# One listed order for a sorted-block attention and its two-layer network: chunk 0's queries on both row halves, keys copied whole, the second sort matrix computed later

## The chip, the core and the metric

The kernel runs on one core of a Trainium2 chip. A core has a matrix engine (TensorE, in the profile PE; its weight loads are shown apart as PEld), a vector engine (VectorE, DVE), an engine for activation functions (ScalarE, ACT), a general engine (GpSimd, POOL) and one that mostly issues transfers (SyncE, SP). Each engine takes its own instructions strictly in the order of the program, and waits on semaphores for what others have to finish first. TensorE reads SBUF and writes PSUM; VectorE and ScalarE move results from PSUM back to SBUF. Transfers are issued from the queues of POOL, SP and ACT; here POOL issues those that also convert float32 to bfloat16.

The metric is device time in microseconds (us) of one execution. The times are those of whole executions; the profile is of one execution and shows its span, from the first instruction to the last.

## The reference: what is computed

There are 4 batches of 8 heads with 768 positions of 64 features. The positions of a head are cut into 8 blocks of 96. A small 8 x 8 matrix per head is normalised five times (softmax along the rows, then division by the column sums), and mixes the blocks of keys and values. Each block of queries then attends to the one mixed block in its place. The result, 3072 tokens of 512 features, goes through a two-layer network with the activation h cos h.

```python
for _ in range(5):
    P = P - max(P, -1); P = exp(P)
    P = P / (sum(P, -1) + 1e-9); P = P / (sum(P, -2) + 1e-9)
k_sorted = einsum('bhij,bhjcd->bhicd', P, k_b); v_sorted = einsum('bhij,bhjcd->bhicd', P, v_b)
attn = softmax(scale * q_b @ k_sorted^T); x = attn @ v_sorted      # per block of 96
h = x @ w_in; out = (h * cos(h)) @ w_out                            # 512 -> 2048 -> 512
```

## The kernel before, in words

**Tiles.** The 3072 tokens are done in 8 chunks of 384: chunk n is batch n // 2, and its half n % 2 of four blocks u = 0 to 3. Per chunk and block the steps are `qk` (scores of 8 heads, maximum and subtraction on DVE), `expo` (the exponential on ACT), the transposition of the probabilities (on PE with a copy, `p_transpose`, for chunks 0 and 1; by a transposing transfer from SP after that), `av` (times the values, and the division on DVE), and the transposition of the result into `xT`. Then come the layers: `moe_up` (16 blocks f of 128 hidden features; PE products `h`, cosine on ACT as a sine with a shift, product `gg` on DVE) and `moe_down` (three tiles of 128 tokens, 16 products of 512 columns each into `o`, a copy and a store).

**Sorting.** `k_sort_0` (batch 0), `k_sort_1` (batch 1) and `k_sort_g` (batches 2 and 3 together) mix the keys by PE products with a block-diagonal matrix `bds`, 16, 8 or 4 positions of a block at a time, and copy the results into `kTs`, from which scores take their moving operand. `v_sort_b` and `v_sort_g` do the same to the values, reading for most of them `vperm`, a copy of the values with features outermost that POOL makes (`v_permute`, about 2.8 us per instruction). The two sort matrices, group 0 (batches 0 and 1) and group 1 (batches 2 and 3), are computed side by side at the start, four rounds each of exponential (ACT), column sums (a float32 product `sk` on PE) and normalisation (four small DVE instructions).

**Zeros.** A score product takes 128 rows: two heads of 64 features. To get one head alone, from chunk 1 on, the queries lie in `q_turned` with zeros in the other head's rows, one copy for each head of a pair (so 8 products of 96 columns per block); POOL writes those zeros (L658 to L661), and the transposing transfer of the queries moves them too. For chunk 0 the products use 64 rows, and `k_sort_0` writes its copies in four parts by row halves.

**What sets the order.** It is written out by hand. The scheduler is off: each engine executes in the order in which the program's calls emit instructions. `moe_up` and `moe_down` take lists of slots; after each step of the layer the calls of one slot are emitted. So a layer's slots decide where the next chunk's attention stands in each engine's queue. PSUM has three buffers of two banks (`big`, called B) and two of one bank (`acc`, C), taken in turn; an instruction that takes a buffer waits until its previous content has been read.

**Start.** POOL issues the loads of chunk 0's queries, batch 0's keys and values, three quarters of `w_in`, then (behind `v_permute`) the last quarter, chunk 1's queries, the four quarters of `w_out`, and batch 1's keys and values. PE begins with 16 products of zeros (`keep_warm`, 25 in all). Chunk 0's first layer begins when two of its four blocks are attended; it is done in two halves of 192 tokens, and the other two blocks, chunk 1's keys and chunk 1's queries stand in its slots. Chunk 1's probabilities, its values and batch 1's keys stand in chunk 0's second layer.

```python
    moe_up(0, [[(p_transpose, 0, 2, V, *C)], [(p_transpose, 0, 3, V, *C)],
               [(av, 0, 2, True), (k_sort_0, 1, 0, 16, A, *C)], [(av, 0, 3, True)],
               [(x_transpose, 0, 2, A, *C)],
               [(x_transpose, 0, 3, A, *C), (k_sort_0, 1, 16, 16, V, *C)],
               [(q_transpose, 1, 0, (V, V), *C)], [(k_sort_0, 1, 32, 16, A, *C)]],
           0, 2 * blk)
```

## Time and profile before

| what | value |
|---|---|
| time, three executions | 246.4, 247.95, 249.35 us (median 247.95) |
| the profiled execution | span 246.5 us; the page gives no other time for it |
| PE busy | 232.0 us, 94% of the span |
| DVE, ACT, POOL busy | 175.5, 158.2, 88.2 us |
| start of chunk 0's first layer | 28.91 us |
| start of chunk 0's second layer | 51.65 us |
| start of chunk 1's first layer | 70.41 us |
| start of chunk 1's second layer | 83.48 us |

The starts are those of the first `h` (L556) or `o` (L580) product in the timeline. The profile is read in this order: the share of each engine over 40 slices, with the TensorE clock that was granted; then the same by the stages of the table; then the groups of instructions with their mean durations; then the chain of work that ended last, which gives the pitch of products that follow each other. A matmul's duration in a group (379 ns for 512 columns) is longer than its pitch (1.73 us for eight), because matmuls overlap.

### The profile page before, as it was taken

The numbers are of one execution on the slowest core, as the hardware profiler recorded it, in microseconds if no ns is written. First come the engines' busy times: TensorE is split into PE (matmuls) and PEld (weight loads), VectorE is DVE, ScalarE is ACT, GpSimd is POOL, SyncE is SP. The second block draws the span as 40 slices with busy tenths as digits, with TensorE's granted clock in tenths as the row PEclk, the third lists the DMA queues.
The fourth block names the chain that finished last, engine by engine and source line by source line (L and its number), as shares of the span: only waits on it lengthen the run. The fifth ranks groups of instructions, "written<-read, shape, count | busy, mean of one in ns | idle before, by whom it ended". The sixth has DMA issues, their size and how long they took to land.

```text
span 246.5 us, 5361 instructions
## 1 busy us (share of the span) xinstructions
PE 232.0 (94%) x2159; PEld 149.5 (61%) x2159; DVE 175.5 (71%) x321; ACT 158.2 (64%) x228; POOL 88.2 (36%) x105
## 2 busy tenths in 40 slices
PE   7987898878999999999999999998999999999994
...
PEclk9555569999999999999999999999999999999999
DMA  4999999994998457946697957986490580133012
GB/s 51 232 192 169 184 205 227 165 210 95 179 214 144 34 138 107 137 103 159 170 106 137 57 128 89 245 53 114 96 245 13 112 169 26 32 83 129 0 45 85
DMA packets 68313, 31.30 MB, mean 127 GB/s; under 512 B 57024, under 2 KB 63808, under 8 KB 68032
## 3 DMA queue, kind: packets, MB, share of 16 engines
...
q10 hardware_dynamic: 512, 0.20, 0.3%
...
## 4 chain that ended last, share of the span: by engine, by line
PE 77%; DVE 8%; ACT 7%; DMA 4%; issue 2%; DVEq 0%; ACTq 0%
PE h L556 33%; PE o L580 26%; PE sc L399 3%; PE av L519 3%; DMA vperm<-p_buf 3%; PE pps L506 2%; ACT p_buf L483 2%; PE ks L346 2%; DVE kTs L286 2%; ACT L483 2%; PE vs L432 1%; DVE gg L563 1%; PE xps L544 1%; PE vs L422 1%; PE sk L258 1%
## 5 line engine op out<-in xcount | busy, mean ns | idle before, releaser
L556 PE MATMUL h<-xT,w_in_t 128*128 128x384 bf16 (+1 forms) x576 | 93.4, 313 | 1.5 <-DVE gg L563 0.8
L580 PE MATMUL o<-w_out_t,gg 128*128 128x512 bf16 x368 | 87.5, 379 | 0.5 <-DVE s L455 0.5
L560 ACT ACTIVATE c<-h,half_pi 128x768 f32<-128x768 f32 (+1 forms) x72 | 59.7, 829 | 30.7 <-PE h L556 28.3
L563 DVE TENSOR_TENSOR gg<-c,h 128x768 bf16<-128x768 f32 (+1 forms) x72 | 61.3, 860 | 24.5 <-ACT c L560 24.5
L556 PEld LDWEIGHTS <-w_in_t 128*128 128x128 bf16 x576 | 53.8, 100 | 28.8 <-issue 2.5
L580 PEld LDWEIGHTS <-gg 128*128 128x128 bf16 x368 | 33.4, 98 | 33.1 <-DVE s L455 0.7
L455 DVE TENSOR_TENSOR s<-sc,mx 96x384 f32<-96x384 f32 (+1 forms) x43 | 32.2, 749 | 2.7 <-DVE mx L454 0.5
L454 DVE TENSOR_REDUCE mx<-sc 96x4 f32<-96x384 f32 (+1 forms) x43 | 31.9, 741 | 2.8 <-PE sc L399 1.9
L177 POOL COPY vperm<-kv 64x1536 bf16<-64x1536 bf16 (+1 forms) x10 | 28.0, 2840 | 1.6 <-DMA kv<-in_v_dram 1.6
L483 ACT ACTIVATE p_buf<-s 96x768 bf16<-96x768 f32 x32 | 27.6, 895 | 0.6 <-DVE s L455 0.2
L528 DVE TENSOR_TENSOR xn<-av,r 96x512 bf16<-96x512 f32 x32 | 22.0, 686 | 1.1
L284 ACT CAST kTs<-ks 128x512 bf16<-128x512 f32 (+2 forms) x31 | 14.1, 456 | 6.1 <-PE ks L346 6.0
L134 POOL DMA_DIRECT2D kv<-in_q_dram x24 | 16.0, 676 | 3.9 <-DMA kv<-in_v_dram 3.2
L399 PE MATMUL sc<-kTs,q_turned 128*128 128x96 bf16 x224 | 16.1, 206 | 0.8 <-DVE s L455 0.7
L526 DVE RECIPROCAL r<-av 96x8 f32<-96x8 f32 x32 | 6.4, 198 | 13.8 <-PE av L519 13.7
L399 PEld LDWEIGHTS <-q_turned 128*128 128x128 bf16 x224 | 12.8, 98 | 4.8 <-DVE s L455 1.3
L284 ACT COPY o_s<-o 128x512 f32<-128x512 f32 (+2 forms) x11 | 5.9, 537 | 14.8 <-PE o L580 11.8
L284 ACT COPY kv<-o 128x512 f32<-128x512 f32 x8 | 4.7, 582 | 14.0 <-PE o L580 14.0
L134 POOL DMA_DIRECT2D q_mem<-in_q_dram x16 | 10.6, 670 | 0.3 <-issue 0.3
L560 ACT ACT_TABLE_LOAD x8 | 10.3, 1283 | 0.1
L284 ACT CAST pair<-vs 96x512 bf16<-96x512 f32 (+1 forms) x12 | 8.7, 727 | 2.0 <-PE vs L432 2.0
L519 PEld LDWEIGHTS <-pT 96*128 96x128 bf16 (+1 forms) x160 | 7.9, 106 | 3.1 <-issue 0.7
...
## 6 DMA issues: line engine op xcount, KB each, us to landing
...
kv<-in_k_dram POOLq DMA_DIRECT2D x2, 768.0 KB, 13.4
kv<-in_v_dram POOLq DMA_DIRECT2D x2, 768.0 KB, 16.6
pair<-in_k_dram POOLq DMA_DIRECT2D x2, 768.0 KB, 12.2
...
```

What stands on the lines that cost most here:

```text
L134: nc.gpsimd.dma_start(out=q_heads[:, i, :, e], in_=src[:, ih * IC + i, :, e])
L177: nc.gpsimd.tensor_copy(dst, src)
L284: eng.copy(dst, src)
L399: nc.tensor.matmul(out, q_of(n, hp)[:, x:x + 128], keys_of(n, u, h2, hp), start=True, stop=True)
L454: nc.vector.reduce_max(mx[:], scv, axis=AX.X)
L455: nc.vector.tensor_tensor(s_t[n, u][:, part[0]:part[0] + w], scv, mx.to_broadcast([blk, w, H2, blk]), op=ALU.subtract)
L483: nc.scalar.activation(dst, src, AF.Exp, scale=scale)
L528: nc.vector.tensor_tensor(xn.rearrange("p h e d -> p e h d"), avv[:, :, :, :D], r.to_broadcast([blk, 2, H2, D]), op=ALU.mult)
L556: nc.tensor.matmul(h[:, f2, :w], w_in_t[:, kk, f * 128:(f + 1) * 128], xT[n][:, kk, lo:hi], start=(kk == 0), stop=(kk == KC - 1))
L560: nc.scalar.activation(c[:, :, :w], h[:, :, :w], AF.Sin, bias=half_pi[:, 0:1])
L563: nc.vector.tensor_tensor(gt[n, fp][:, :, lo:hi], c[:, :, :w], h[:, :, :w], op=ALU.mult)
L580: nc.tensor.matmul(o[:], gt[n, f // 2][:, f % 2, ts * 128:(ts + 1) * 128], w_out_t[:, f, :], start=(f == 0), stop=(f == FC - 1))
```

## The change

The hand-written calls and slots are replaced by one list, `PLAN`, of 657 small steps, each a short text with its arguments: the letter V or A is the engine of a copy, B or C the PSUM pool. The program goes through it and calls the step's function, so an engine's order is the order of the list. `ld_` steps are loads on POOL, `z_` steps fill zeros and constants, `w N` is N products of zeros of 256 columns, `b_` steps are the sort matrix of one group, `up n f0 nf lo hi` is nf hidden blocks of the first layer for tokens lo to hi of chunk n, `dn n ts part` a quarter (four products) of the second layer's tile ts. Beside the order, these things change:

- The first loads are batch 0's values, then chunk 0's queries, then the keys; the quarters of the weights are in the order w_out 3, w_out 1, w_in 0, chunk 1's queries, w_out 2, w_in 2, w_in 1, w_in 3, w_out 0. Chunk 1's queries have a buffer of their own.
- Chunk 0: queries (`q0`) and sorted keys (`k0`) lie on both row halves, so that each sorting group is one copy of 128 rows instead of four of 64, and a score tile is made of 16 products of 48 columns.
- All of chunk 0's attention, batch 0's remaining keys and chunk 1's queries stand ahead of the first `up`. The first layer of chunk 0 goes by four hidden blocks of 192 tokens, in the order of the list.
- From chunk 1 on the zeros lie in the keys (`kP0`, `kP1`, `kPg`, four slots for a pair of heads), the queries are kept once (one transposing transfer instead of two), and a block's scores are 4 products of 192 columns. Two slots of the keys are filled by PE and a copy, two by transfers from SP (`ksw`), and the zeros by POOL (`z_k`), the last two of them after the transfers.
- The sort matrix of group 1 is computed at the end of chunk 0's second layer and the start of chunk 1's first, instead of at the start.
- Chunk 2's queries are turned by a transfer instead of 32 PE transpositions and four copies.
- 122 products of zeros instead of 25: 72 ahead of the first keys' products, 40 between these and the first `up`, and 10 within chunk 0's first layer.

```diff
+PLAN = [
+    "ld_s", "z_warm", "ld_v 0", "z_id", "z_k 0 1", "z_pi", "w 4 B", "w 20 C", "b_max 0", "z_tail",
+    "b_exp0 0", "b_ci 0", "z_mask", "ld_qr 0", "b_rows 0", "ld_k 0", "ld_wo 3", "ld_wo 1", "b_turn 0",
+    "z_same", "z_order", "ld_wi 0", "w 10 B", "ld_qr 1", "w 3 C", "b_cols 0", "hold cs 0", "b_ci 0",
+    "b_exp 0", "b_sum 0", "z_p 2", "b_inv 0", "b_norm 0", "w 1 C", "w 5 B", "z_p 1", "b_ci 0", "b_exp 0",
+    "w 2 C", "b_sum 0", "b_inv 0", "b_norm 0", "b_ci 0", "w 1 B", "w 11 B", "w 1 C", "b_exp 0", "b_sum 0",
+    "z_p 0", "w 5 C", "w 2 C", "b_inv 0", "b_norm 0", "b_ci 0", "q0 3 V B", "w 1 C", "b_exp 0", "b_sum 0",
+    "b_inv 0", "b_norm 0", "b_ci 0", "ld_wo 2", "b_end 0", "q0 0 V B", "vp 0 48 16", "w 6 B", "q0 1 V B",
+    "b_max 1", "k0 0 0 16 A C", "k0 0 32 16 V B", "b_v", "q0 2 V B", "k0 0 16 16 A C", "z_pad", "w 7 C",
+    "qk 0 1 2 B", "v0 2 0 8 A B", "ld_wi 2", "qk 0 0 2 B", "mx 0 1 2", "w 4 C", "v0 2 8 8 A C", "w 4 C",
+    "v0 2 56 8 A B", "v0 2 48 8 A C", "mx 0 0 2", "z_ones 0", "qk 0 3 2 B", "mx 0 3 2", "ex 0 1 0",
+    "v0 2 24 8 V C", "w 2 B", "ex 0 0 0", "v0 2 40 8 A C", "pp 0 1 V B", "b_exp0 1", "qk 0 2 2 B",
+    "pp 0 0 A B", "w 4 C", "v0 2 16 8 A B", "z_k 0 0", "ld_wi 1", "v0 2 32 8 A C", "mx 0 2 2", "w 7 C",
+    "ex 0 2 0", "ld_wi 3", "ld_wo 0", "av 0 1", "w 2 C", "pp 0 2 V C", "av 0 0", "k0 1 0 16 A C",
+    "k0 1 16 16 V B", "w 3 C", "ex 0 3 0", "av 0 2", "k0 1 32 16 V C", "ksw 0 0", "pp 0 3 A B", "z_k 0 2",
+    "w 2 C", "xp 0 0 A B", "w 1 B", "xp 0 1 A C", "xp 0 2 V B", "ld_q 2 0", "qp 1 0 V B", "qp 1 1 V C",
+    "w 4 B", "av 0 3", "up 0 8 4 0 192", "ld_k 1", "up 0 0 4 0 192", "xp 0 3 A C", "up 0 12 4 0 192",
+    "up 0 0 4 192 384", "up 0 4 4 192 384", "ksw 0 1", "z_k 0 3", "w 2 C", "qk 1 0 1 C", "mx 1 0 1",
+    "qk 1 0 0 B", "mx 1 0 0", "up 0 4 4 0 192", "up 0 8 4 192 384", "qk 1 1 0 C", "ld_v 1", "w 8 C",
+    "mx 1 1 0", "up 0 12 4 192 384", "qk 1 2 2 B", "ld_kg 1 2", "ld_kg 0 2", "ld_q 2 1", "ld_q 2 2",
+    "qk 1 1 1 C", "ld_q 2 3", "vp 2 16 16", "dn 0 0 0", "mx 1 1 1", "mx 1 2 2", "dn 0 0 1", "dn 0 0 2",
+    "vp 2 0 16", "dn 0 0 3", "vp 1 48 16", "ex 1 0 0", "ex 1 1 0", "z_k 1 0", "vp 2 32 16", "ld_vg 4 6",
+    "qk 1 3 2 B", "oc 0 0 A 0", "st 0 0 S", "pp 1 0 V C", "pp 1 1 A B", "ld_vg 5 6", "ld_vg 0 6",
+    "k1 8 8 A B", "z_k 1 1", "ld_vg 3 6", "ex 1 2 0", "mx 1 3 2", "dn 0 1 0", "k1 16 8 V B", "ld_vg 1 6",
+    "ex 1 3 0", "dn 0 1 1", "av 1 1", "pp 1 2 V B", "dn 0 1 2", "b_ci 1", "k1 32 8 A B", "k1 40 8 V C",
+    "k1 24 8 V B", "k1 0 8 A B", "dn 0 1 3", "oc 0 1 A 0", "st 0 1 S", "av 1 0", "ksw 1 0", "z_k 1 2",
+    "av 1 2", "pp 1 3 V C", "dn 0 2 0", "dn 0 2 1", "xp 1 1 A B", "av 1 3", "dn 0 2 2", "dn 0 2 3",
+    "b_rows 1", "b_turn 1", "b_cols 1", "ksw 1 1", "z_k 1 3", "b_ci 1", "b_exp 1", "v1 32 8 A B", "qd 2",
+    "oc 0 2 A 0", "b_sum 1", "ld_vg 2 6", "b_inv 1", "b_norm 1", "b_ci 1", "xp 1 3 V C", "xp 1 0 V B",
+    "b_exp 1", "b_sum 1", "v1 8 8 A C", "ld_q 3 1", "st 0 2 S", "b_inv 1", "b_norm 1", "b_ci 1", "b_exp 1",
+    "xp 1 2 V B", "v1 24 8 A B", "v1 40 8 A C", "b_sum 1", "b_inv 1", "b_norm 1", "b_ci 1", "b_exp 1",
+    "ld_q 3 3", "up 1 6 2 0 384", "up 1 2 2 0 384", "v1 0 8 A C", "up 1 10 2 0 384", "b_sum 1", "b_inv 1",
+    "b_norm 1", "ld_q 3 2", "up 1 0 2 0 384", "up 1 12 2 0 384", "v1 56 8 A C", "qk 2 0 0 C", "mx 2 0 0",
+    "up 1 4 2 0 384", "ld_q 3 0", "v1 16 8 A C", "qk 2 0 1 B", "mx 2 0 1", "up 1 8 2 0 384", "qd 3",
...
-    def scores(out, n, u, h2, hp):
-        x = (u * H2 + h2) * blk
-        if n == 0:
-            rows = slice(hp * D, (hp + 1) * D)
-            nc.tensor.matmul(
-                out[:blk], q_of(0, 0)[rows, x:x + blk], keys_of(n, u, h2, hp)[rows],
-                start=True, stop=True)
-        else:
-            nc.tensor.matmul(
-                out, q_of(n, hp)[:, x:x + 128], keys_of(n, u, h2, hp), start=True, stop=True)
...
-    def k_sort_0(ih, t0, nt, eng, pool, tag):
...
-        for hp in range(2):
-            for x in range(2):
-                copy_on(eng, kT[0][hp * D:(hp + 1) * D, hp + x, ms, ts],
-                        psv[x * D:(x + 1) * D, hp])
...
-    for it in range(4):
-        for g in range(NG):
-            nc.scalar.activation(E[g][:], T[g][:], AF.Exp, scale=ci[g][:])
...
-        sk = [product(same, E[g]) for g in range(NG)]
...
-    for t in (q_turned[1], q_turned[0]):
-        nc.gpsimd.memset(t[64:, 0], 0.0)
-        nc.gpsimd.memset(t[:64, 1], 0.0)
...
-    moe_up(0, [[(p_transpose, 0, 2, V, *C)], [(p_transpose, 0, 3, V, *C)],
...
-    moe_down(0, [[(qk, 1, 2), (p_transpose, 1, 0, A, *B), (k_sort_1, 0, V, *B)],
...
+    kP1 = const.tile([128, 4, NB, HT], BF16, name="kP1")
+    kPg = const.tile([128, 4, 2 * NB, HT], BF16, name="kPg")
+    early_keys = kPg.rearrange("p s m t -> p (s m t)")
+    k0s = early_keys[:, :2 * MH * HT].rearrange("p (e m t) -> p e m t", e=2, m=MH)
+    q0d = early_keys[:, 1536:1536 + 2 * QW]
+    kP0 = early_keys[:, 6144:6144 + 4 * MH * HT].rearrange("p (s m t) -> p s m t", s=4, m=MH)
+    spare = early_keys[:, 9216:9984].bitcast(FP32).rearrange("p (z x j) -> p z x j", z=3, j=nb)
+    L, same = [spare[:, 0], spare[:, 1]], spare[:, 2]
+    bdv = early_keys[:, 9984:10112].rearrange("p (x j) -> p x j", j=nb)
+    order = early_keys[:blk, 10112:10112 + blk]
...
+    def z_k(g, part):
+        t, (rows, s) = KP[g], ((slice(64, 128), 1), (slice(0, 64), 2),
+                               (slice(64, 128), 0), (slice(0, 64), 3))[part]
+        G.memset(t[rows, s], 0.0)
...
+    def w(times, pool):
+        idle = pool[0].tile([128, 256], FP32, name="idle", tag=pool[1])
+        for _ in range(times):
+            nc.tensor.matmul(
+                idle[:], warm[:], warm[:, :1].to_broadcast([128, 256]), start=True, stop=True)
...
+    def q0(z, eng, pool):
+        ps = pool[0].tile([128, 2, IC, QR, blk // QR], BF16, name="qps", tag=pool[1])
+        for e in range(2):
+            for r in range(QR):
+                src = q_mem[:, 0, ((z * 2 + e) * QR + r) * D:((z * 2 + e) * QR + r + 1) * D]
+                for x in (0, 64):
+                    nc.tensor.transpose(ps[x:x + 64, e, :, r], src, ident[:blk, :blk])
+        dst = q0d.rearrange("d (i h c) -> d h i c", h=H, c=blk)[:, z * 2:z * 2 + 2]
+        copy_on(eng, dst, ps.rearrange("d e i r p -> d e i (r p)"))
...
+    def k0(ih, t0, nt, eng, pool):
+        ps = pool[0].tile([128, nt, 2, MH], FP32, name="ks", tag=pool[1])
+        rows = slice(64, 128)
+        for t in range(nt):
+            nc.tensor.matmul(
+                ps[:, t], k_pos(t0 + t, kbuf, rows), bds[0][64:, H:, ih * IC:(ih + 1) * IC],
+                start=True, stop=True)
+        dst = k0s[:, :, :, t0:t0 + nt] if ih == 0 else kP0[:, ::3, :, t0:t0 + nt]
+        copy_on(eng, dst, ps.rearrange("p t e m -> p e m t"))
...
+    def ksw(g, z):
+        t = KP[g]
+        if z == 0:
+            nc.sync.dma_start(out=t[:64, 1], in_=t[64:, 0])
+        else:
+            nc.sync.dma_start(out=t[64:, 2], in_=t[:64, 3])
...
+    def scores(n, u, h2, out):
+        g, b2, ih = where(n)
+        if n == 1:
+            keys = kP0[:, :, h2 * IC + u]
+        else:
+            m = h2 * nb + ih * IC + u
+            keys = kP1[:, :, m] if g == 0 else kPg[:, :, b2 * NB + m]
+        c = (u * H2 + h2) * blk
+        nc.tensor.matmul(
+            out, q_turned[n % 2][:, c:c + 128], keys, start=True, stop=True)
...
+    def qk(n, u, part, pool):
+        zs = (0, 1) if part == 2 else (part,)
+        sc = pool[0].tile([128, len(zs), 512], FP32, name="sc", tag=pool[1])
+        if n == 0:
+            for a in range(H):
+                for x in range(2):
+                    rows, c = slice(x * 64, x * 64 + 64), (u * H + a) * blk
+                    nc.tensor.matmul(
+                        sc[:blk, x, a * HT:(a + 1) * HT], q0d[rows, c:c + blk],
+                        k0s[rows, a % 2, a // 2 * IC + u], start=True, stop=True)
+            sc_t[n, u, part] = sc
+            return
+        for j, z in enumerate(zs):
+            for x in range(2):
+                scores(n, u, z * 2 + x, sc[:, j, x * 2 * blk:(x + 1) * 2 * blk])
+        sc_t[n, u, part] = sc
...
+    def mx(n, u, part):
+        zs = (0, 1) if part == 2 else (part,)
+        w = len(zs)
+        if (n, u) not in s_t:
+            s_t[n, u] = sp.tile([blk, 2, H2, blk], FP32, name="s", tag="s")
+        scv = sc_t.pop((n, u, part))[:blk, :, :H2 * blk]
+        if n == 0:
+            scv = scv.rearrange("p x (a t) -> p a x t", t=HT)
+            m = small.tile([blk, H], FP32, name="mx", tag="mx")
+            V.reduce_max(m[:], scv, axis=AX.XY)
+            V.tensor_tensor(
+                s_t[n, u].rearrange("p z a (t x) -> p (z a) x t", x=2), scv,
+                m[:].unsqueeze(2).to_broadcast([blk, H, 2, HT]), op=ALU.subtract)
+            return
+        scv = scv.rearrange("p z (a c) -> p z a c", c=blk)
+        m = small.tile([blk, w, H2], FP32, name="mx", tag="mx")
+        V.reduce_max(m[:], scv, axis=AX.X)
+        dst = s_t[n, u][:, zs[0]:zs[0] + w]
+        if n < ROWS:
+            for j in range(w):
+                V.tensor_tensor(
+                    dst[:, j].rearrange("p a (t x) -> p a x t", x=2),
+                    scv[:, j].rearrange("p a (x t) -> p a x t", x=2),
+                    m[:, j].unsqueeze(2).to_broadcast([blk, H2, 2, HT]), op=ALU.subtract)
+        else:
+            V.tensor_tensor(dst, scv, m.to_broadcast([blk, w, H2, blk]), op=ALU.subtract)
...
+    def up(n, f0, nf, lo, hi):
+        h = big.tile([128, 2, 512], FP32, name="h", tag="big")
+        w = hi - lo
+        hv = [h[:, f * 2 // nf, f * 2 % nf // 2 * w:(f * 2 % nf // 2 + 1) * w] for f in range(nf)]
+        for f in range(nf):
+            for kk in range(KC):
+                nc.tensor.matmul(
+                    hv[f], w_in_t[:, kk, (f0 + f) * 128:(f0 + f + 1) * 128],
+                    x_of(n)[:, kk, lo:hi], start=(kk == 0), stop=(kk == KC - 1))
+        half = nf // 2
+        hh = h[:, :, :half * w]
+        c = cosp.tile([128, 2, TC], FP32, name="c", tag="c")
+        cc = c[:, :, :half * w]
+        A.activation(cc, hh, AF.Sin, bias=half_pi[:, 0:1])
+        at = g_at(n, f0)
+        dst = gall[:, at:at + nf, lo:hi]
+        if half > 1:
+            dst = dst.rearrange("p (z f) c -> p z f c", z=2)
+            cc = cc.rearrange("p z (f c) -> p z f c", f=half)
+            hh = hh.rearrange("p z (f c) -> p z f c", f=half)
+        V.tensor_tensor(dst, cc, hh, op=ALU.mult)
...
+    def dn(n, ts, part):
+        if part == 0:
+            out_ps[n, ts] = acc.tile([128, Dm], FP32, name="o", tag="acc")
+        for f in range(part * FC // 4, (part + 1) * FC // 4):
+            nc.tensor.matmul(
+                out_ps[n, ts][:], gall[:, g_at(n, f), ts * 128:(ts + 1) * 128], w_out_t[:, f, :],
+                start=(f == 0), stop=(f == FC - 1))
...
+    for call in PLAN:
+        name, *args = call.split()
+        args = [POOL[a] if a in POOL else a for a in args]
+        if name == "st":
+            args[2] = QUEUE[args[2]]
+        args = [ENG[a] if isinstance(a, str) and a in ENG else a for a in args]
+        args = [int(a) if isinstance(a, str) and a.isdigit() else a for a in args]
+        calls[name](*args)
```

778 lines of the change are left out of this document (264 added, 514 removed), and 52 rows, old and new, of the table PLAN.

## The prediction

> **What bounds the kernel now.** The page comes first: the busy tenths of 40 slices, the granted clock, the transfers, and the chain that ended last.
>
> ```profile
> span 246.5 us, 5361 instructions
> ...
> PE   7987898878999999999999999998999999999994
> ...
> PEclk9555569999999999999999999999999999999999
> DMA  4999999994998457946697957986490580133012
> ...
> PE 77%; DVE 8%; ACT 7%; DMA 4%; issue 2%; DVEq 0%; ACTq 0%
> ```
>
> PE is 77% of the chain and full from the twelfth slice on. Before that it has gaps, its clock is at half in slices 2 to 6, and the transfers are at 90% or more for nine slices. So I ask the same by stages, cut where the first key product, the first `h`, the first `o`, and so on begin.
>
> ```profile
> 0.00:13.18 13.18, 11.33 (x79) 8.39 (x80) 7.60 (x51) 6.07 (x17) 6.50 (x17) 0.78 0.82 146
> 13.18:28.91 15.73, 12.10 (x187) 10.62 (x186) 13.21 (x26) 13.12 (x24) 14.07 (x14) 0.50 1.16 178
> 28.91:51.65 22.74, 19.94 (x264) 17.28 (x264) 16.58 (x35) 13.29 (x27) 14.73 (x13) 0.87 1.12 200
> 51.65:70.41 18.76, 17.25 (x224) 10.87 (x224) 12.42 (x24) 11.46 (x17) 16.48 (x18) 1.00 0.87 160
> 70.41:83.48 13.07, 13.07 (x148) 8.78 (x146) 10.85 (x17) 11.22 (x16) 11.78 (x7) 1.00 1.09 145
> 83.48:246.50 163.02, 158.30 (x1268) 93.53 (x1265) 114.87 (x172) 103.05 (x130) 24.66 (x38) 1.00 0.57 105
> ```
>
> The columns are the length, PE, PEld, DVE, ACT and POOL busy, the clock, the DMA share and GB/s. From 83.48 PE is busy 158.3 of 163.0 us, and its products stay the same; little can be won there. From 13.18 to 28.91 no engine is full, the clock is 0.50, DVE and ACT hand work to and fro. What the change is worth is decided in the first 83.48 us. I rebuild the five stages one after the other.
>
> **Stage 1, up to the first `h` (28.91).** It is set by the arrival of the keys and then by DVE.
>
> ```profile
> 2.02 0.91 POOL L124 DMA_DIRECT2D q_mem<-in_q_dram  x1
> 2.92 0.56 POOL L93 DMA_DIRECT2D kv<-in_k_dram  x1
> 3.45 0.55 POOL L93 DMA_DIRECT2D kv<-in_v_dram  x1
> ...
> 25.32 0.60 POOL L93 DMA_DIRECT2D kv<-in_v_dram  x1
> ```
>
> ```profile
> kv<-in_k_dram POOLq DMA_DIRECT2D x1, 768.0 KB, 8.1
> kv<-in_v_dram POOLq DMA_DIRECT2D x1, 768.0 KB, 11.4
> ...
> kv<-in_v_dram POOLq DMA_DIRECT2D x1, 768.0 KB, 21.9
> ```
>
> These are times of issue, and us from issue to landing for the last three of them: keys land at 11.0, values at 14.85, batch 1's values at 47.2. Queries, keys and values together are there 12.8 us after POOL starts its first load at 2.02. In the new list that load stands ahead of the constants, about 1.2 us earlier, so all three are there by about 13.6; but the keys are now last. Between 14.85 and 47.2 the queue, never empty, landed eight quarters of weights, chunk 1's queries, and batch 1's keys and values (3.6 each, between the 3.85 of the values and a little less for the keys): 2.6 per quarter if queries take 4.3, 2.9 if they take 2. In the new order w_in 3, which is used third, is behind seven quarters and the queries: 13.6 + 22.5 = 36.1.
>
> The sort matrix of group 0 alone goes round in the time of the two below, four times, and is done near 13, no later than the keys.
>
> ```profile
> 5.75 0.40 PE sk L258 x2
> ...
> 7.35 0.61 PE sk L258 x2
> ...
> 17.20 0.55 PE sc L394 x8
> ...
> 28.91 1.44 PE h L556 x8
> ...
> 50.48 0.67 PE h L556 x8
> ...
> 69.65 0.83 PE qps L298 x32
> ...
> 71.89 0.47 PE vs L422 x16
> ...
> 87.66 0.34 PE sc L399 x8
> ```
>
> These are pieces of the chain in order of time (start, length, how many). From the first key product (13.18) to the first score took 4.0 us. Now three copies of 128 rows replace the parts by row halves, with a query copy and 7 fillers between: between 2.7 and 4.0, I take 3.4, which puts DVE's first maximum at 17.0. From there DVE has an unbroken list, by these groups of the whole span:
>
> ```profile
> L563 DVE TENSOR_TENSOR gg<-c,h 128x768 bf16<-128x768 f32 x56 | 52.7, 949 | 18.6 <-ACT c L560 18.6
> L528 DVE TENSOR_TENSOR xn<-av,r 96x512 bf16<-96x512 f32 x32 | 22.0, 686 | 1.1
> L455 DVE TENSOR_TENSOR s<-sc,mx 96x768 f32<-96x768 f32 x21 | 20.0, 954 | 1.9 <-DVE mx L454 0.5
> L454 DVE TENSOR_REDUCE mx<-sc 96x8 f32<-96x768 f32 x21 | 19.9, 946 | 2.8 <-PE sc L399 1.9 <-PE sc L394 0.9
> L455 DVE TENSOR_TENSOR s<-sc,mx 96x384 f32<-96x384 f32 x22 | 12.2, 553 | 0.8
> L454 DVE TENSOR_REDUCE mx<-sc 96x4 f32<-96x384 f32 x22 | 12.0, 546 | 0.0
> ...
> L526 DVE RECIPROCAL r<-av 96x8 f32<-96x8 f32 x32 | 6.4, 198 | 13.8 <-PE av L519 13.7
> ...
> L286 DVE CAST kTs<-ks 128x512 bf16<-128x512 f32 x3 | 2.0, 681 | 1.8 <-PE ks L346 1.8
> ...
> L286 DVE COPY pT<-pps 96x768 bf16<-96x768 bf16 x2 | 1.1, 546 | 0.0
> ```
>
> Four maxima and subtractions 4 x 1.90 = 7.6; four `av` divisions 4 x 0.88 = 3.5; three copies of 512 elements, 2.0; two of `pT`, 1.1; three smaller or equal ones, 1.5: 15.7, plus 0.5 where it waits: 33.2. The new strided maximum and subtraction of chunk 0 have no row; they move as many elements, and I take the same (not under 1.90; at twice that for one of them, 4 us more). The first `up` stands just ahead of DVE's last division: **32.8, 3.9 later than before**. It has taken along two blocks of attention, three key groups and chunk 1's queries.
>
> **Stage 2, chunk 0's first layer (22.74 before).** PE: 128 products at 0.67 / 8 make 10.7; scores of three sets, 1.0; 10 fillers of 256 columns at 0.112, 1.1; a transposition, 0.2: 13.0. It arrives at w_in 3 about 0.4 before it lands. DVE needs 8 x 0.949 + 4 x 1.10 = 12.0 behind 33.2 and a first pause of some 1.7 until the first cosine is there, so the buffer that the last score tile needs comes free at about 47. I take 14.4 for the stage: `dn` begins at **47.2, 4.45 earlier**.
>
> A wait is added here. POOL's `z_k 0 2` waits for the first key swap, since it zeros what the swap reads; behind it stand the first quarter of chunk 2's queries, batch 1's keys and `z_k 0 3`, and chunk 1's first scores on PE wait for that, with the rest of the layer behind them.
>
> ```profile
> L664 POOL MEMSET kTs<- 64x1536 bf16 x1 | 1.4, 1371 | 0.1
> ```
>
> ```profile
> kTs<-kTs SPq DMA_DIRECT2D x2, 384.0 KB, 4.4
> kTs<-kTs SPq DMA_DIRECT2D x2, 192.0 KB, 7.8
> ```
>
> The swap is issued near 31.6; on SP only the sort matrices' load stands ahead of it. 7.8 was measured under a full queue with twice the bytes, 4.4 in a half-empty one: it lands between 36.0 and 39.4; two memsets of half L664's size and two issues of about 0.6 later it is 38.6 to 42.0. PE gets there at about 40: between nothing and 2.0. I take nothing, as the bytes are half; 2.0 is kept for the range.
>
> **The clock** decides what the same products take: eight of 192 columns took 1.44 at 28.91 and 0.67 at 50.48. At half clock the first four groups of eight would cost 4 x 0.77 = 3.1 more. Before, PE was busy 77% from 13.18 to 28.91 and the clock stayed at 0.50; in the rows with 92% (51.65) and above it is 1.00. 40 fillers of at least 0.112 add 4.5 us to the 12.1 of a stage of this kind, which is nearer the second rows, so I take the full clock.
>
> [...]
>
> **Stage 3, chunk 0's second layer (18.76 before).** Gone are 32 query transpositions (0.83) and one score set (0.34). Added are four value groups moved ahead (2 x 0.47), three products `sk` (0.9), and the sort matrix of group 1: three rounds of 1.6 (5.75 to 7.35), each covered by 0.2 to 0.8 of values and transpositions on PE; DVE and ACT queue copies among its steps. That leaves 2.0 open, bounded by 0 (all covered) and 4.8 (none). Of the 1.5 in which PE was idle before I let half go, as three of four score sets are ready ahead. 18.76 - 0.83 - 0.34 + 0.94 + 0.9 + 2.0 - 0.8 = **20.6**, so the next layer begins at 67.8.
>
> **Stage 4, chunk 1's first layer (13.07 before).** Four value groups fewer (0.94), two score sets more (0.68), one more `sk` (0.4): **13.2**, to 81.0.
>
> **Stage 5 (163.02 before).** The two score sets are gone: **162.3**. Four products of 192 columns cost 4 x 0.67 / 8 = 0.34, as much as eight of 96. Half the query transposition and fewer loads shorten the queues of SP and POOL beside a full PE, which waits for neither; four larger zero fills lie on POOL, busy 24.7 of 163.0. These I put at nothing; without that cover they would hold up later queries by some 3 us.
>
> **Sum.** 81.0 + 162.3 = 243.3 against the span of 246.5: 3.2 less. The page has no other time for that execution; the runs (246.4 to 249.35) begin at its span, so I add nothing around it and take the 3.2 from their median: 247.95 - 3.2 = 244.75, rounded **244.8**.
>
> **The rivals.**
> - *Half clock until chunk 0's first layer.* For it: the half clock at 77% busy. Against: the fillers. Price 3.1: 247.9.
> - *The second sort matrix lies bare, or the swap is late.* For it: DVE and ACT have copies between its steps. Against: PE has work listed between the rounds. Price 2.0 to 2.8 each: about 247.3.
> - *Better overlap.* The 2.0 of stage 3 and the 1.4 of stage 2 beyond PE's own 13.0 vanish: 241.4.
> - *Slower: chunk 0's chain pays a hand-over at each step.* All four blocks now stand ahead of the first `h`, in one list across four engines. If each of DVE's 16 steps waits 0.37 for PE or ACT instead of running back to back, the first `up` comes at 38.8, and nothing behind is shortened by that: 244.8 + 6 = 250.8. It decides when DVE's idle time there passes about 6 us. For it: 13.8 us of waits at the reciprocal L526. Against: between 13.18 and 28.91 DVE was idle only 2.5.
> - *The change is not what it says:* the order on each engine is the list's, so I give this nothing.
>
> **Chances.** Forecast 0.45, half clock 0.18, bare sort matrix or late swap 0.05, better overlap 0.12, slower 0.20. The forecast's own range is 243 to 246.5. A measurement of this kernel tells about 1% from no change, 245.5 to 250.4; of the forecast some 0.10 lies within it. Faster 0.47, same 0.33, slower 0.20. The range from 241.2 to 250.8 takes in all cases up to the middle of the slower one.
>
> **What will show it.** Right: PEclk without fives in slices 3 to 6; the first `h` near 32.8, `o` near 47, chunk 1's `h` near 68, its `o` near 81; DVE over 90% busy from 17 to 33. Wrong: the first `h` after 35, PE waiting for a memset or a swap before chunk 1's scores, waits at `sk` of more than 1 us each near 65, or a last stage longer than 164.

## The result and the profile after

The changed kernel takes **257.89 us** in the median of four runs (256.84 to 265.46), the kernel before 247.94 beside it: a ratio of 1.038 (95% interval 1.030 to 1.046), **slower** by some 4%. The forecast was 244.8, with a range up to 250.8. The executions of one kernel differ in length (a1 below ran from 250.0 us at a mean granted clock of 0.99 to 262.7 at 0.95), so a ratio is taken over those within 1.5% of the kernel's fastest, which leaves out 265.46 here and eight of a1's eleven, and stages are compared between profiled executions.

The page of the profiled execution (span 255.1, time 256.84), the same lines as before; the two lines under the transfers are the chain that ended last, by engine and by line.

```profile
span 255.1 us, 5327 instructions
...
PE   8799999999979999799999999999999999999994
...
PEclk9998555999999999999999999999999999999999
DMA  6999981999299934925697945793490442053012
...
PE 80%; DVE 7%; ACT 5%; DMA 5%; issue 2%; DVEq 0%; ACTq 0%
PE h L614 28%; PE o L636 26%; PE idle L310 6%; PE av L575 3%; DVE gall L628 2%; PE sc L497 2%; DMA vperm<-p_buf 2%; PE vs L460 2%; PE pps L565 2%; DMA pT<-p_buf 2%; PE xps L601 2%; PE vs L479 1%; ACT c L621 1%; PE ks L413 1%; DVE mx L534 1%
```

PE is now full from the third slice on but for two sevens, where before it had gaps up to the tenth. The fives of the clock have moved to slices 5 to 7. And "PE idle L310" is no idleness: `idle` is the tile into which the filler products of the steps `w` write, and they are 6% of the chain that sets the end.

By stages, cut at the first key product, the first `h`, the first `o`, chunk 1's `h` and its `o` (columns as in the prediction):

```profile
0.00:16.22 16.22, 13.31 (x130) 10.15 (x131) 7.86 (x32) 3.22 (x9) 14.31 (x25) 1.00 0.93 159
16.22:42.56 26.34, 26.14 (x394) 22.28 (x391) 16.55 (x30) 13.07 (x22) 0.78 (x2) 0.63 0.98 162
42.56:56.82 14.26, 13.62 (x157) 13.13 (x156) 10.49 (x16) 7.66 (x10) 8.73 (x11) 0.97 0.93 170
56.82:76.10 19.28, 17.70 (x220) 11.64 (x220) 14.97 (x39) 11.23 (x19) 16.62 (x13) 1.00 0.90 156
76.10:90.34 14.24, 13.42 (x116) 8.75 (x116) 10.42 (x22) 11.75 (x17) 9.17 (x8) 1.00 1.12 149
90.34:255.10 164.76, 157.90 (x1168) 92.45 (x1168) 114.51 (x171) 102.09 (x130) 30.76 (x28) 1.00 0.51 94
```

| ends at | before | forecast | after | after's stage against its forecast |
|---|---|---|---|---|
| first key product | 13.18 | 13.6 | 16.22 | +2.6 |
| stage 1, first `h` | 28.91 | 32.8 | 42.56 | +9.8 with the line above |
| stage 2, first `o` | 51.65 | 47.2 | 56.82 | -0.1 |
| stage 3, chunk 1's `h` | 70.41 | 67.8 | 76.10 | -1.3 |
| stage 4, chunk 1's `o` | 83.48 | 81.0 | 90.34 | +1.0 |
| stage 5, end of the span | 246.5 | 243.3 | 255.1 | +2.5 |

The last column adds up to the 11.8 us between forecast and measured span. The time up to the first `h` holds 9.8 of them; stages 4 and 5 add 3.5, and stages 2 and 3 give 1.5 back. The second row of the fence says what stage 1 is bound by: from the first key product to the first `h` PE is busy 26.14 of 26.34 us. Before, the same stretch had PE at 12.10 of 15.73. Three things in it stand out.

**A step of the sort matrix is held up by a copy.** DVE's list, then POOL's, around the third round:

```profile
9.56 0.21 DVE L349 RECIPROCAL rr<-sk 128x8 f32<-128x8 f32 x1 [0.87 <-PE sk L321]
9.91 2.04 DVE L352 CUSTOM_DVE_ANT_0 T<-E,rr 128x8 f32<-128x8 f32 x1
11.89 0.08 DVE L352 DVE_READ_ACCUMULATOR2_ANT cs<- 128x1 f32 x1
```

```profile
9.11 2.81 POOL L452 COPY vperm<-kv 64x1536 bf16<-64x1536 bf16 x1
```

A DVE product of 8 elements per row takes 2.04 us and ends (11.95) when POOL's copy `vp 0 48 16` ends (9.11 + 2.81 = 11.92). The reciprocal ahead of it, started while the copy ran, takes its usual 0.21. In the kernel before, POOL first read one column of the second sort matrix, and copied then:

```profile
14.32 0.19 POOL L336 CAST held<-bd 128x1 f32<-128x1 bf16 x1 [4.50 <-DVE bd L278]
14.90 2.76 POOL L177 COPY vperm<-kv 64x1536 bf16<-64x1536 bf16 x1 [0.38 <-DMA kv<-in_v_dram]
```

The new list has no such wait.

**Fillers at half clock.** PE's pieces of four fillers each, early and late in stage 1:

```profile
20.86 0.62 PE L310 MATMUL idle<-warm 128*128 128x256 bf16 x4
...
22.23 0.62 PE L310 MATMUL idle<-warm 128*128 128x256 bf16 x4
...
28.56 1.05 PE L310 MATMUL idle<-warm 128*128 128x256 bf16 x4
```

The same four products go from 0.62 to 1.05. The clock falls at about 23 us, on a PE that is all but never idle; here is the stretch in which it does:

```profile
20.00:24.00 4.00, 3.98 (x68) 3.42 (x68) 3.31 (x4) 1.90 (x4) 0.00 (x0) 0.87 1.35 202
```

**POOL stands still** for 24.7 us ahead of `z_k 0 2`, which waits for the key swap, and the transfers all but run dry from 36 to 44 us:

```profile
POOL kPg L305 <- DMA kPg<-kPg: 24.7, 1, 24.7
```

### The profile page after: what moved, and what is told of

It reads as the page before. It is cut to its first block, busy times and chain, and to the rows that moved or that the text cites. A ratio compares the mean times of both kernels' runs of the same rounds, so it can differ in the third digit from the quotient of the medians.

```text
span 255.1 us, 5327 instructions
## 1 busy us (share of the span) xinstructions
PE 242.1 (95%) x2176; PEld 158.4 (62%) x2176; DVE 174.8 (69%) x307; ACT 149.0 (58%) x204; POOL 80.4 (32%) x83
## 4 chain that ended last, share of the span: by engine, by line
PE 80%; DVE 7%; ACT 5%; DMA 5%; issue 2%; DVEq 0%; ACTq 0%
PE h L614 28%; PE o L636 26%; PE idle L310 6%; PE av L575 3%; DVE gall L628 2%; PE sc L497 2%; DMA vperm<-p_buf 2%; PE vs L460 2%; PE pps L565 2%; DMA pT<-p_buf 2%; PE xps L601 2%; PE vs L479 1%; ACT c L621 1%; PE ks L413 1%; DVE mx L534 1%
## 5 line engine op out<-in xcount | busy, mean ns | idle before, releaser
L636 PE MATMUL o<-w_out_t,gall 128*128 128x512 bf16 x368 | 87.2, 379 | 2.0 <-DVE s L543 1.4
L628 DVE TENSOR_TENSOR gall<-c,h 128x768 bf16<-128x768 f32 x64 | 60.1, 949 | 23.8 <-ACT c L621 23.7
L621 ACT ACTIVATE c<-h,half_pi 128x768 f32<-128x768 f32 x64 | 57.6, 902 | 29.3 <-PE h L614 28.5
L636 PEld LDWEIGHTS <-gall 128*128 128x128 bf16 x368 | 34.0, 98 | 35.4 <-DVE s L543 1.9
L452 POOL COPY vperm<-kv 128x1536 bf16<-128x1536 bf16 (+1 forms) x9 | 25.6, 2878 | 10.7 <-DMA kv<-in_v_dram 5.5
L305 POOL MEMSET kPg<- 64x768 bf16 (+1 forms) x8 | 13.5, 1690 | 36.6 <-DMA kPg<-kPg 36.4
L310 PE MATMUL idle<-warm 128*128 128x256 bf16 x122 | 21.9, 330 | 1.0 <-DVE half_pi L276 1.0
L582 DVE RECIPROCAL r<-av 96x8 f32<-96x8 f32 x32 | 6.4, 199 | 19.3 <-PE av L575 19.2
L310 PEld LDWEIGHTS <-warm 128*128 128x128 bf16 x122 | 13.2, 118 | 4.2 <-DVE half_pi L276 1.0
L214 ACT CAST kPg<-ks 128x512 bf16<-128x512 f32 x15 | 8.7, 582 | 9.0 <-PE ks L413 6.0
L214 ACT CAST vS<-vs 96x512 bf16<-96x512 f32 x15 | 8.5, 583 | 5.6 <-PE vs L460 4.8
L214 ACT COPY xT<-xps 128x384 bf16<-128x384 bf16 x11 | 5.3, 479 | 10.5 <-PE xps L601 10.4
## 6 DMA issues: line engine op xcount, KB each, us to landing
pair<-in_k_dram POOLq DMA_DIRECT2D x2, 768.0 KB, 14.4
```

The lines of the kernel that those rows point to most:

```text
L214: A.copy(dst, src)
L310: nc.tensor.matmul(idle[:], warm[:], warm[:, :1].to_broadcast([128, 256]), start=True, stop=True)
L452: G.tensor_copy(dst, src)
L621: A.activation(cc, hh, AF.Sin, bias=half_pi[:, 0:1])
L628: V.tensor_tensor(dst, cc, hh, op=ALU.mult)
L636: nc.tensor.matmul(out_ps[n, ts][:], gall[:, g_at(n, f), ts * 128:(ts + 1) * 128], w_out_t[:, f, :], start=(f == 0), stop=(f == FC - 1))
```

## The experiments

All are edits of the changed kernel's list. Boundaries of most of their profiled executions, in us:

| run | first key product | first `h` | first `o` | chunk 1's `h` | its `o` | chunk 2's `h` | end |
|---|---|---|---|---|---|---|---|
| before | 13.18 | 28.91 | 51.65 | 70.41 | 83.48 | 97.96 | 246.5 |
| after | 16.22 | 42.56 | 56.82 | 76.10 | 90.34 | 105.63 | 255.1 |
| a1 copy held | 14.15 | 41.88 | 56.23 | 76.11 | 92.22 | 107.51 | 258.7 |
| a2 no late fillers | 16.24 | 36.66 | 52.27 | 71.76 | 87.04 | 102.33 | 253.5 |
| a3 no fillers | 16.37 | 37.51 | 52.08 | 71.79 | 93.70 | 110.71 | 261.0 |
| a4 loads first | 16.25 | 40.77 | 54.77 | 74.05 | 88.30 | 103.58 | 253.2 |
| b1 = a1 + a2 + a4, no later fillers | 14.12 | 34.76 | 50.13 | 69.42 | 83.67 | 101.37 | 250.3 |
| b2, 16 early fillers | 14.30 | 35.43 | 51.28 | 70.64 | 86.20 | 101.48 | 250.1 |
| b3 late fillers doubled | 16.21 | 40.53 | 54.35 | 73.70 | 89.26 | 104.55 | 254.6 |
| c1 = b1, both copies held | 14.76 | 35.33 | 51.04 | 70.33 | 84.58 | 99.87 | 248.6 |
| c3 only both copies held | 14.29 | 34.54 | 48.37 | 68.52 | 83.46 | 98.75 | 248.6 |

### Three suspects one by one

a1, the copy waits for the first sort matrix:

```diff
-"vp 0 48 16"
+"hold bd 0", "vp 0 48 16"
```

> Edit: POOL's first block copy of the values waits for the finished sort matrix of group 0 instead of standing inside its rounds. Theory (the copy on POOL holds up DVE's two-input step, 2.04 us instead of 0.17): that step takes under 0.3 us, the first key product starts near 14.3 instead of 16.22, the first layer near 40.7 instead of 42.56, and the time is 1.5 to 2 us less (ratio near 1.031). Rival (the step is long for a reason of its own): it stays above 1.5 us, time within 0.5 us of the changed kernel. Second rival (PE is the bound behind it and its clock falls as much earlier): the first key product is 1.9 us earlier but the first layer less than 1 us.

The step takes 0.17 us and the first key product comes at 14.15, 2.1 earlier. DVE's row of the same round in a1:

```profile
9.67 0.17 DVE L354 CUSTOM_DVE_ANT_0 T<-E,rr 128x8 f32<-128x8 f32 x1
```

In the five profiled executions without the wait it took 1.78 to 2.39 us; it began between 9.58 and 10.20 and always ended within 0.05 us of the copy's end. In all ten with the wait it took 0.17. The profiled execution (260.48) has its first `h` only 0.7 earlier than the changed kernel: the clock falls near 19 us in it instead of 23 (four fillers take 1.03 us at 19.16), which is the outcome of the second rival. The ratio is 1.009 (1.004 to 1.013) where 1.031 was expected, but by the three shortest of eleven executions; the median of all is 254.09 beside 249.04 for the kernel before. So the copy is shown as a cause, its price of 2 us is shown up to the first key product, and the spread says that something larger varies behind it. The price could hardly be more: the keys land at 13.9 to 14.4 in the profiled executions (issued at 3.92, 10.0 to 10.5 to landing), so a faster sort matrix can bring the first key product little ahead of 14.15.

a2, the 40 fillers between the first key product and the first `h` left out; a3, all 122:

```diff
-"w 7 C", "w 4 C", "w 4 C", "w 2 B", "w 4 C", ... (to the first "up")
```

> Edit: the 40 filler products between chunk 0's first key product and its first layer are left out (their results are used by nothing). Theory (PE is the bound there: it is busy in 26.2 of the 26.4 us from 16.2 to 42.6, and the fillers take 9.0 us of that): the first layer starts 5 to 9 us earlier, at 34 to 38, and the time is 249 to 253. Rival (DVE's chain of hand-overs is the bound and the fillers only fill PE's waits): the first layer stays at 41.5 to 43, time 256 to 258. Third (the fillers buy clock): the granted clock falls to 0.50 before 18 us instead of near 20 and the gain is under 4 us.

> Edit: all 122 filler products are left out (their results are used by nothing). Theory (fillers are a cost on PE's list everywhere in the first stage): beside the 5 to 9 us behind the key products, the sort matrix's first product comes about 1 us earlier (6.02 to near 5), and the first key product 1 to 2 us earlier; first layer at 32.5 to 36.5, time 247 to 251.5. Rival (the fillers are what keeps the granted clock at full up to 20 us): the clock is 0.50 until the first layer, the key products and scores of chunk 0 take twice as long, and the result is no better than with the 72 early fillers kept.

a2: 255.59, ratio 1.025 (1.021 to 1.030). The first `h` is 5.9 earlier, as the theory of a full PE had it. The time is above its 249 to 253, and the span only 1.6 shorter: the clock is at half from 20 us on (0.50 from 20 to 36), the second stage takes 15.6 instead of 14.3, and stage 4 has a dip of the clock (0.91 in its row, 15.3 instead of 14.2). a3: 1.036 (1.028 to 1.044), no gain at all. Its sort matrix starts 0.85 earlier (5.17 against 6.02), yet the first key product is no earlier, and the first `h`, at 37.5, misses the expected 32.5 to 36.5. In stage 4 of the profiled execution (262.73) PE waits for the turned queries of chunk 2, a DMA on SP that takes 19.9 us to land, 11.8 in the changed kernel:

```profile
PE sc L496 <- DMA q_turned<-q_mem: 4.7, 1, 4.7
```

The early start is not shown to be the reason: a2 reaches the same point at the same time (71.76 against 71.79), issues that DMA 0.2 later, and has no such wait. The page of a3 also teaches how far the clock's row can be trusted. The row of the stage, and the length of single score products of chunk 0 (least, median, most, in ns) in a3 and in c3 (below):

```profile
16.37:37.51 21.14, 19.70 (x352) 18.42 (x351) 16.15 (x30) 12.63 (x22) 0.74 (x1) 1.00 1.20 195
```

```profile
L507 PE MATMUL sc<-kPg x64: 194/251/273, 19.5 to 26.5; 64*96 64x48 bf16 x64
```

```profile
L511 PE MATMUL sc<-kPg x64: 199/199/220, 17.1 to 24.7; 64*96 64x48 bf16 x64
```

Both executions show a granted clock of 1.00 there, yet a3's products take 251 against 199. b2 below has the same contradiction: 1.00, with 16 such products in 0.83 us as in a3, where c3 takes 0.54. It would fit a row that begins at full and shows only changes, since a3's first two products of the sort matrix already take 0.59 us together instead of c3's 0.28; no run shows how the row is made. The length of a product of known shape is the safer reading.

a4, the loads behind POOL's long wait go ahead of it:

```diff
-"z_k 0 2", ..., "ld_q 2 0", ..., "ld_k 1", ..., "ld_v 1"
+"ld_v 1", "ld_q 2 0", "ld_k 1", "z_k 0 2", ...
```

> Edit: on POOL's list the loads of chunk 2's first queries, of batch 1's keys and of batch 1's values go ahead of the memset that waits 24.7 us for the key swap. Theory (that wait empties the DMA queues between 32 and 44 us and makes chunk 1's values and the loads behind them late): the first layer stays at 42.6 within 0.5, values of batch 1 land over 8 us earlier than 54.7, stages 3 to 5 lose 1 to 2.5 us and the time is 255 to 257 in the mean (ratio 1.028 to 1.034). Rival (nothing waits for those loads on the path): no difference above 0.5 us.

Ratio 1.026 (1.019 to 1.032), which overlaps the changed kernel's 1.030 to 1.046: a gain, if any, is small. The stages say more: 2, 3 and 4 take 14.0, 19.3 and 14.25 against after's 14.26, 19.28 and 14.24. The value copies that wait for that load start at 51.9 instead of 54.7, not the 8 us earlier that I expected, and nobody on the path waits for them. Its first `h` is 1.8 earlier, in an execution whose clock fell near 27 us instead of 23 (four fillers take 0.62 us at 22.22 and 0.97 at 26.93). The dry queue, the most striking thing on the page, cost nothing. POOL itself still stands idle in a4, 16.7 us for DVE; in the changed kernel PE's only listed wait in stage 2 is 0.5 us for DVE's subtraction.

### Together, and the clock

b1 joins the three edits and also leaves out the 10 fillers within the first layer. b2 is b1 with only 16 of the 72 early fillers. b3 takes the changed kernel as it is and doubles the 40 late fillers. b4 is b1 with the first layer's first two steps ahead of the third block:

```diff
 b2: -"w 4 B", "w 20 C", "w 10 B", "w 3 C", ...   +"w 4 B", "w 12 C"
 b3: -"w 7 C", "w 4 C", ...   +"w 14 C", "w 8 C", ...
 b4: -"xp 0 2 V B", "qp 1 0 V B", "qp 1 1 V C", "av 0 3", "up 0 8 4 0 192", "up 0 0 4 0 192", "xp 0 3 A C"
     +"up 0 8 4 0 192", "av 0 3", "up 0 0 4 0 192", "xp 0 2 V B", "xp 0 3 A C", "qp 1 0 V B", "qp 1 1 V C"
```

> Edit: the copy held, the 50 fillers from chunk 0's first key product on left out, the loads ahead of the waiting memset, all three together (the 72 early fillers stay). Theory (each removes a cost of its own on PE's list): first key product 14.1 to 14.3, first layer 33.5 to 36, first output product 48 to 51, time 248 to 252.5, at best level with the kernel before. Rival (the clock falls earlier as PE's list empties, and gives the gain back): first layer as in the run without fillers less 2 us, but the time above 253.

> Edit: as the run before it, and of the 72 early fillers only 16 stay, ahead of the first maximum (the kernel before has as many). Theory (24 fillers ahead of the sort matrix's first product make it 1 us late): its first product at 4.6 to 5.3 instead of 5.8 to 6.1, first key product 13 to 13.7, time 0.5 to 1.5 us under the run before it. Rival (the early fillers buy the granted clock behind them): clock 0.50 from the start of the key products, first layer no earlier than with 72, time the same or above.

> Edit: on the changed kernel the 40 filler products between chunk 0's first key product and its first layer become 80. Theory (PE is the bound there, fillers stand on its list): first layer 6 to 9 us later than 42.56, at 48.5 to 51.5, time 261 to 266. Rival (twice as many keep the granted clock at full, and the other products there run at twice the rate): clock above 0.9 from 20 to 42 us, first layer at 40 to 43, time 254 to 258.

> Edit: as the first run of this group, and the first two steps of chunk 0's first layer stand right behind the turned outputs of its first two blocks, with the third block's output and chunk 1's query turns behind them. Theory (PE is the bound from the key products to the first output product, so its order there is worth little): first layer 2 to 3 us earlier than in the first run of this group, first output product within 1 us of it, time within 1 us. Rival (ScalarE's table change and cosines are late next): first output product and time 2 to 3 us earlier.

b1: 251.41 in the median, 1.013 (1.006 to 1.019), inside the theory's figures. b2: 1.017 (1.009 to 1.025), no gain: the sort matrix starts at 5.03, but its products run at half clock, here in b2 and in a1:

```profile
8.58 0.60 PE L321 MATMUL sk<-E,kPg 128*128 128x8 f32 x2 [1.50 <-ACT E L343]
```

```profile
12.24 0.29 PE L323 MATMUL sk<-E,kPg 128*128 128x8 f32 x2
```

The matrix is done at 13.93 (13.73 in b1), and the first key product at 14.30 waits for the keys' DMA: the fewer fillers win nothing there, and what the others cost can't be read from it. b4: 1.016 (1.011 to 1.021); its first `h` is only 0.4 earlier than b1's, not 2 to 3, its first `o` 1.8 later. Order alone was worth nothing there.

b3 is the telling one. Its stage 1 and stage 2:

```profile
16.21:40.53 24.32, 23.98 (x434) 21.23 (x431) 16.20 (x30) 12.93 (x22) 0.98 (x2) 1.00 1.07 175
40.53:54.35 13.82, 13.18 (x159) 12.74 (x156) 10.49 (x16) 7.64 (x10) 7.86 (x11) 1.00 0.93 171
```

With 40 products **more** the first `h` comes 2.0 us **earlier**, at 40.53: the rival's outcome. Here the clock is truly at full, by the length of the fillers themselves:

```profile
23.61 1.06 PE L312 MATMUL idle<-warm 128*128 128x256 bf16 x8
...
28.95 1.05 PE L312 MATMUL idle<-warm 128*128 128x256 bf16 x8
```

As a remedy it is none: the ratio is 1.036 (1.028 to 1.044), and two executions with a lower mean clock (0.96 and 0.95 against 0.99) took 261.7 and 277.3. What makes the clock fall is not settled.

### The copies once more

b1's profile shows 17.7 us from chunk 1's `o` to chunk 2's `h`, after only 15.3. DVE's list there:

```profile
83.53 0.94 DVE L629 TENSOR_TENSOR gall<-c,h 128x768 bf16<-128x768 f32 x1
84.39 2.98 DVE L360 SCALAR_TENSOR_TENSOR bd<-maskp,ci,T 128x128 bf16<-128x128 f32 x1
87.30 0.54 DVE L535 TENSOR_REDUCE mx<-sc 96x4 f32<-96x384 f32 x1
```

```profile
78.80 11.26 POOL L453 COPY vperm<-kv 128x1536 bf16<-128x1536 bf16 x4 [3.87 <-PE vs L471]
```

The spread of the second sort matrix, 0.34 us in the changed kernel, takes 2.98. The four copies of some 2.86 begin at 78.80; the third starts with the spread, at 84.4, and ends with it, near 87.3. (a3's profile has the same: 2.28 for the spread, ending with the third copy, and 17.0 for the stretch.) In the changed kernel the same step began 5.60 us behind the first of the four copies, where the second ends and the third starts, and slipped in; here it came as near and missed. c1 adds a wait of these copies for that matrix; c2 also forms the output of chunk 2's last block earlier; c3 puts only the two waits into the changed kernel:

```diff
 c1, c3: -"vp 2 16 16"                +"hold bd 1", "vp 2 16 16"     (the second half's)
 c2:     -"dn 1 2 3", ..., "av 2 3"   +"av 2 3", "dn 1 2 3"
```

> Edit: the run with held copy, no late fillers and loads first, and POOL's four value copies for the second half also wait for the second sort matrix. Theory (a copy on POOL holds up DVE's two-input steps: there the spread of the second sort matrix took 2.98 us instead of 0.34 and ended with the copy): that step 0.34 to 0.36, from chunk 1's first output product to chunk 2's first layer 15.3 us instead of 17.7, time 248 to 250.5, ratio 1.000 to 1.008. Rival (the copies, now late, make the value sort of the second half late): the step is short but the wait for the copies shows on PE ahead of the second half's value products, time 250.5 or more.

> Edit: as the run before it, and the output of chunk 2's last block is formed one output product part earlier. Theory (PE's idle time of 1.3 us ahead of chunk 2's first layer is the chain from that output through DVE, turn and copy): 0.7 to 1.2 us less from chunk 1's first output product to chunk 2's first layer, time 247.2 to 249.5, ratio 0.995 to 1.004. Rival (the transfer of its turned weights lands only then): PE waits at that output instead, no gain.

> Edit: on the changed kernel alone, both groups of value copies wait for their sort matrix (two waits added, all fillers kept). Theory (clock and fillers are the larger part of the loss in the first layer, the copies 2 us of it in the sort matrix): first key product near 14.2, first layer 38 to 41 as the granted clock falls, time 250 to 256 with the spread that the clock gives; the second spread 0.35 us. Rival (the copies are all of it): time within 1 us of the kernel before.

c1: the spread is back at 0.34, and the stretch at 15.3. Time 251.78, ratio 1.014 (1.009 to 1.019), no better than b1 and above what was expected: PE shows no wait for the late copies, which the rival asks for; the mishap of b1's profile seems not to be that of its median run. c2: 1.014 (1.009 to 1.018), the stretch 15.2, so a gain of 0.1 where 0.7 to 1.2 were expected. c3: **252.57, ratio 1.013 (1.007 to 1.020)**. Two waits alone, with all fillers, give as much as everything in c1; its first `h`, at 34.54, comes earlier than the 38 to 41 that I expected, since the clock held (four fillers take 0.61 to 0.62 us all through the stage). Its stages from the first key product on, in the shortest of its four executions:

```profile
14.29:34.54 20.25, 19.79 (x394) 17.27 (x391) 15.95 (x30) 12.33 (x22) 7.01 (x7) 1.00 1.26 201
34.54:48.37 13.83, 13.18 (x160) 12.74 (x156) 10.58 (x17) 8.15 (x11) 6.65 (x10) 1.00 0.86 156
48.37:68.52 20.15, 18.46 (x220) 12.13 (x220) 15.76 (x39) 11.41 (x20) 17.39 (x12) 0.97 1.06 184
68.52:83.46 14.94, 14.25 (x116) 9.01 (x116) 10.51 (x22) 11.77 (x16) 5.57 (x7) 0.93 1.06 148
83.46:248.60 165.14, 158.07 (x1168) 92.33 (x1168) 114.53 (x171) 102.00 (x130) 35.43 (x30) 1.00 0.52 94
```

and beside it the first stage of a2, without late fillers and at half clock:

```profile
16.24:36.66 20.42, 18.98 (x354) 17.76 (x351) 15.99 (x30) 12.61 (x22) 0.74 (x1) 0.59 1.24 203
```

Four executions whose work from key product to `h` differs only in the fillers, and in the copies on POOL that c3 has moved into it, answer the question of stage 1. 40 fillers at full clock (c3): 20.25. None, at half clock from 20 us on (a2): 20.42. 80 at full clock (b3): 24.32, 40 fillers or 4.07 us more, 0.102 each. And 40 at a clock that falls to half on the way (after, 0.50 from 24 to 36): 26.34. Taking away either fault, the fall of the clock or the fillers, is worth 6 us. The other profiles fit: d2 below, 40 fillers at full clock, takes 20.20; a4, 40 fillers and a fall near 27 us, 24.52; those without late fillers in the same order, at half clock for most of the stage or all of it, 20.2 to 21.8. No run has neither fault, so what 40 fillers cost at full clock is not shown; in c3 PE is still busy 19.79 of 20.25 us with them. How much of c3's gain is the clock alone isn't shown: a4, without the waits, had a late fall too, and with the same 40 fillers the clock held in c3 and d2 (four fillers in 0.61 to 0.62 us) but fell in after, a1, a4 and, for some 7 us, in d1 (1.05, 1.03, 0.97 and 1.05).

### What is left in stages 4 and 5

c3 reaches its first `o` 3.3 us ahead of the kernel before and ends 2.1 behind it. Of the 5.4 lost, 1.4 lie in stage 3 (20.15 against 18.76), 1.9 in stage 4 (14.94 against 13.07, with a dip of the clock to 0.93 in its row) and 2.1 in stage 5 (165.14 against 163.02). PE's idle time ahead of chunk 1's and chunk 3's first output product was put down to DVE's subtraction of the scores, which frees a PSUM buffer that the first output product takes. d1 (on c3) and d3 (on c1) move these score tiles; d2 is d1 with 16 instead of 24 fillers at the very start:

```diff
-"qk 2 1 1 C", "qk 2 2 2 B", ..., "dn 1 0 0"      +"qk 2 1 1 B", "dn 1 0 0", "qk 2 2 2 B", ...
-"qk 4 1 1 C", "mx 4 1 1", ..., "vg 60 4 A C"      +"vg 60 4 A C", "qk 4 1 1 C", "mx 4 1 1", ...
```

> Edit: both groups of copies held, all fillers kept, and ahead of chunk 1's and chunk 3's first output product the score tile that this product's PSUM buffer has to wait for goes elsewhere (chunk 2's second half score to the other pool behind the first output part; the last value product of chunk 3 ahead of chunk 4's second half score). Theory (PE's idle 0.6 and 0.8 us there is that buffer, freed by DVE's subtraction): those two waits under 0.2 us, stage 4 and the stage of chunk 3 each 0.5 to 1 us shorter, time 0.8 to 1.8 us under the run with the copies held alone, 249.5 to 252 in the median, ratio 1.003 to 1.011. Rival (the first output product waits for the first layer's products of DVE anyway): the wait changes its name and stays, gain under 0.3 us.

> Edit: as the run before it, and the fillers ahead of the sort matrix's first product are 16 instead of 24. Theory (they stand ahead of that product on PE's list): that product 0.7 to 1 us earlier, the first key product at 13.3 to 13.6, the time 0.5 to 1 us less. Rival (16 don't bring the granted clock to full before the rounds, whose products then take 0.60 us instead of 0.29): the first key product at 14 to 14.6, no gain.

> Edit: both groups held, the 50 late fillers out, the loads first, and the two score tiles moved as in the first run of this group. Theory: first layer near 35 at half the clock, first output product near 51, and 0.8 to 1.8 us under the run without the moved tiles: 249.5 to 251, ratio 1.003 to 1.011, with a narrower spread than with the fillers kept. Rival: as in the first run of this group, gain under 0.3 us.

d1: 1.020 (1.016 to 1.023), d2: 1.021 (1.017 to 1.025), d3: 1.016 (1.011 to 1.020); none is better than its base (d2's executions go up to 264.0, with a median of 257.25). In d3 the wait of 0.6 ahead of chunk 1's first output product is gone, that stage takes 13.66 instead of 14.25, and the next one 17.17 instead of 15.29; part of this only moves the boundary, since two score sets now stand behind the first `o`, but the two together are 1.3 longer. Waits there in c1 and then in d3:

```profile
PE o L638 <- DVE s L545: 0.6, 1, 0.6
```

```profile
PE sc L499 <- DVE gall L630: 1.1, 1, 1.1
```

The wait has changed its name, as the rival said; in chunk 3 it turned from 0.8 for DVE's subtraction into 1.0 for ScalarE's copy. Freeing the buffer does not win the time. In d2 the first product of the sort matrix is at 5.03 and the first key product at 14.18, in d1, with eight fillers more, at 5.05 and 14.17: no difference to be had. Both wait for the keys, in d1 and then in d2:

```profile
14.17 0.96 PE L416 MATMUL ks<-bd,kv 64*128 64x32 bf16 x32 [0.27 <-DMA kv<-in_k_dram]
```

```profile
14.18 0.96 PE L416 MATMUL ks<-bd,kv 64*128 64x32 bf16 x32 [0.27 <-DMA kv<-in_k_dram]
```

## Why the prediction was wrong

**Stage 1, "PE gets the full clock because 40 fillers make it busy"**: this is the step that failed. I used the fillers as the reason for the full clock and gave them no time of their own on PE's list, as if they lay in its gaps. They don't: PE was busy 26.14 of 26.34 us. Even in the stage that I compared with, 4.5 us of fillers don't fit into 15.73 us of which 12.1 were busy, and PE's own list was never added up: 354 products without the fillers (a2's row), where the stage before had 187. And the clock fell in spite of them, so the rest of the list and the fillers ran at half. Together 6 us (26.34 against 20.25 in c3). A high busy share was no warrant for the clock: 26.14 of 26.34 went with 0.63. The 19.2 that I worked out for DVE's list, from the first key product to the first `h`, came near what is measured as soon as one of the two faults is gone (20.25 in c3, 20.42 in a2), but in part by luck: there too PE was the full engine, busy 19.79 and 18.98 us, and DVE only 15.95 and 15.99. The first rival had the fact (half clock) at a price of 3.1, worked out on the first layer's products alone; what stood ahead of them on PE was not counted.

**Stage 1, "the sort matrix goes round in the time of before, done near 13"**: failed, 15.86. Of the 2.9, 1.9 are the copy on POOL beside DVE's step (2.04 instead of 0.17), which I hadn't looked for; for the first key product it is 2.1 (a1: 14.15). The order of POOL's list showed that the copy's wait was gone; I counted its time and not what ran beside it. The rest goes with a first product of the sort matrix at 6.02 instead of 4.39, behind 24 fillers that take 5 of the first 6 us (5.17 without them, in a3; 5.05 with the same 24 in d1, where they took 4.12 us):

```profile
0.00:6.00 6.00, 5.00 (x24) 3.56 (x25) 2.29 (x10) 2.01 (x5) 4.88 (x13) 1.00 0.59 101
```

This rest is not on the path: with the copy held the matrix is done at 13.8 (a1), and the keys, forecast for 13.6, land only at 13.9 to 14.4.

The traces show what the step ran beside. The product (`T<-E,rr`, 2.04 us) and the spread (`bd<-maskp,ci,T`, 2.98 us in b1) each ended with a copy on POOL, and in b2 the same product took 0.17 us beside a memset on POOL:

```profile
7.75 0.17 DVE L352 CUSTOM_DVE_ANT_0 T<-E,rr 128x8 f32<-128x8 f32 x1 [0.43 <-POOL held L376]
```

```profile
7.59 0.87 POOL L267 MEMSET p_buf<- 96x256 bf16 x3
```

In the kernel before, the last spread ends at 14.18 and the first value copy starts at 14.90, so its trace shows no such step beside a value copy. From the 2.04 and 0.17 of the new trace, the removed wait alone would have been a rival of about +2 us, an estimate.

**DVE "over 90% busy from 17 to 33"**: it was not.

```profile
19.60:33.30 13.70, 13.50 (x159) 11.14 (x159) 8.69 (x11) 7.33 (x13) 0.00 (x0) 0.62 1.27 205
```

8.69 of 13.70, while PE has 13.50. My sign for "wrong", the first `h` after 35, was met.

**The slower rival**, a hand-over at each of DVE's 16 steps, named the right stage, the right side, and a sign that came true: DVE's idle time there was 26.34 - 16.55 = 9.8, above 6. Its mechanism was not the one. DVE waited for a full PE; with the fillers out or the clock up its idle time was 4.3 to 4.4 (20.25 - 15.95, 20.42 - 15.99).

**Stage 2**, 14.4: right (14.26). The wait added at `z_k 0 2`, taken as nothing, was 24.7 us long on POOL, and PE shows no wait for it. **Stage 3**, 20.6: 19.28; the 2.0 for a bare sort matrix were too much, what the second rival feared didn't come. **Stage 4**, 13.2: 14.24, with PE idle for 0.8 where before it was never idle.

**Stage 5**, 162.3: 164.76, beyond my sign of 164. PE's work shrank as forecast (157.90 against 158.30), its idle time grew from 4.7 to 6.9. In c3 it is the same, 165.14 with 7.1 idle, so it isn't a consequence of the late start. I had written that PE waits for neither SP nor POOL there; in fact the kernel before lists 1.2 us of waits for SP's transfers, and the changed one 1.1, so that is not what grew. Its listed waits for DVE are 2.5 where before has none, and the costliest is that of the output products:

```profile
L636 PE MATMUL o<-w_out_t,gall 128*128 128x512 bf16 x368 | 87.2, 379 | 2.0 <-DVE s L543 1.4
```

d3 removes these two waits by moving the score tiles and gains nothing. What it would take to win these 2 us back stays open; no version run here beats the kernel before.
